# Two attentions on one core: where TensorE's waits for small transfers are placed, and the place of one PSUM bank in its ring

## The chip, the cores and the metric

The kernel runs on one core of one Trainium2 chip, in one launch. The metric is the device time of one execution in microseconds, taken as the median of several runs; lower is better. Everything is computed in float32, much of it in pairs of a high and a low part.

## The reference

Two independent attention layers over 2048 positions, with 576 channels and 32 heads of 18 channels; their outputs stand side by side in the result. A is local: each position looks at 8 keys, at distances 0, 2, ... 14. B is full.

```python
def A(x, wqkv, wo):                       # B, S, D = 1, 2048, 576;  H, Dh, W, dil = 32, 18, 8, 2
    q, k, v = split(x @ wqkv)             # each (B, H, S, Dh)
    idx = pos[:, None] - (arange(W) * dil)[None, :]
    kg, vg = k[:, :, idx], v[:, :, idx]   # (B, H, S, W, Dh), masked where idx < 0
    logits = einsum("bhsd,bhswd->bhsw", q, kg) * Dh ** -0.5
    o = einsum("bhsw,bhswd->bhsd", softmax(where(mask, logits, -1e9)), vg)
    return o.reshape(B, S, D) @ wo

def B(x, wqkv, wo):
    q, k, v = split(x @ wqkv)
    p = softmax(einsum("bhqd,bhkd->bhqk", q, k) * Dh ** -0.5)
    return einsum("bhqk,bhkd->bhqd", p, v).reshape(B, S, D) @ wo

return concatenate([A(...), B(...)], axis=-1)
```

## The kernel before

**Staging.** A first stage computes the projections of both layers (`stream`, `halves`) and leaves q, k, v in DRAM (`dqk`, `dv` for B, `da` for A). It takes the first 420 us or so (the first value product starts at 423.3). Then comes the main loop, which is 512 steps long (`ALL`) and is B's attention: 8 groups of 4 heads (`g`), in each 4 blocks of 512 queries (`b`), in each 16 tiles of 128 keys (`kt`), one step for each tile. A's local attention is done piece by piece beside the steps, and so are both output products.

**A step on TensorE.** For the four heads `h` of the group, `score` (L277) multiplies the tile's keys with the block's 512 queries into a bank of PSUM; ScalarE takes the exponential of it (L283). The scores of the step before, thus exponentiated, are then multiplied with the values by `weigh` (L748): four *value products*, one for each head, which are added up in one bank, `po`, over the 16 steps of a block.

**The maxima.** The softmax subtracts each query's maximum before the exponential. It does so inside the score itself: rows 54 and 55 of the queries' tile `qs` hold the negated maximum, in a high and a low part, and the keys have ones there. So the maxima of a block must be known before its first step, and they are computed several steps ahead (`AHEAD`) from scores of their own: 128 queries against 512 keys, which VectorE reduces. A step has room for three of these. Two are whole ones (`maximum(0)`, called A below, and `maximum(1)`, called B; matmul L157, reduction L173 or L175). The third is made of two *parts* of 256 keys each, which share a bank: D, the first part (`first_part`, L263 and L264), and E, the second. D and E lie in different halves of TensorE's rows, and before E stands a `nop` (L183) that waits for D, since both write one bank. One reduction (L190) takes both. A plain step's matmuls stand in this order: D, score 1, A, score 3, score 0, E, score 2, B, and then the four value products of the step before.

When all of a block's maxima are there, `least` takes the last reduction over them, `turn` transposes the result on VectorE one step later, `halve` splits it on GpSimd one step later into the high and low part (`mh`, `mt`), and `place` (L214 to L219) writes them, five steps later (two in the last group), into rows 54 and 55 of `qs` by eight small loads of 2 KB, first the four of `mh` (an index `j` for each), then the four of `mt`. The score that opens the block in question comes later, sometimes by a few steps and sometimes by more than a hundred.

**A beside the steps.** A's positions come in 8 tiles of 256 (`local(j)`), one every 54 steps (`GAP`) from step 10 on. GpSimd does nearly all the products, VectorE the maxima over the window (`am`, L903) and its sums. The result goes to DRAM (`dao`), and `get` (L946 to L958) loads it again, with the channels in the partitions, by six loads, as *rows* for the output product: `at0`, `at1`, `ahl`. That product, `sums_of_a`, is run 7 to 10 steps after `get`, in two halves, by `beside` (L1052), in the middle of a step's scores.

**Order.** All is issued in the order of the program (a manual schedule), so each engine runs its instructions in the order in which the Python code comes to them. `plan` and `later` put a function on the `agenda` for a step, and `due` runs it at that step's end, after the value products. A transfer is issued from SyncE's queue (`load`). Each instruction waits for what it reads and writes, and where it waits for several other queues, the additional waits stand as instructions of their own just ahead of it in its engine's queue.

**Banks.** PSUM has eight banks: `po` and seven that go round in rings (L77). In the main loop the scores use ring "scores" (banks 0 to 3), maxima and parts use ring "else" (banks 4 to 6). `bank` takes the ring's first bank and moves it to the end. So in a plain step D takes the bank that the parts had one step before, A and B theirs.

**The last group.** From step 448 on, the outputs of B's older groups are fetched back: `fetch_old` (L1015) puts eight loads of 252 KB in the queue for each of four blocks of queries, and `full` and `partial` plan the output products with them.

Of the kernel before, what the change touches and what calls it, by code (L numbers as in the profile page):

```python
# [7 lines left out]
F32 = mybir.dt.float32  # L8
# [9 lines left out]
D = 576  # L18
# [5 lines left out]
NT = S // 128  # L24
# [4 lines left out]
AB = 256  # L29
# [10 lines left out]
EARLY = 2  # L40
EARLY_PAIRS = EARLY * NB * PIECES + 2
AHEAD = 7

GAP = 54

# [14 lines left out]
def two_attentions(ctx: ExitStack, tc, xa, wa, woa, xb, wb, wob, out):  # L60
# [83 lines left out]
                for d, m in pieces or ((0, DH),) for n, i in enumerate(parts) for r in range(2)]  # L144


    def block(g, b):

        qs, ks = sets[g % 3]
        mx = maxes.tile([128, 2, 2, 4, 6], F32, name="mx", bufs=3)  # L150
        left = 2 * 8 * 6
        rest = [[(k, t, p) for k in range(NB) for t in range(4) for p in range(2)] for _ in range(2)]

        def take(ps, r, k, t, p, at, n):

            rows_ = slice(64 * r, 64 * r + 54)
            return nc.tensor.matmul(ps, qs[rows_, b, p, 128 * t : 128 * t + 128],  # L157
                                    ks[rows_, p, 512 * k + at : 512 * k + at + n], start=True, stop=True)

        def made(n):  # L160
            nonlocal left
            left -= n
            if left == 0:
                least()

        def whole(r):
            k, t, p = rest[r].pop(0)
            ps = bank()
            take(ps, r, k, t, p, 0, 512)

            def reduce():
                if k < 2:
                    nc.vector.tensor_reduce(mx[:, r, p, t, k : k + 1], ps, axis=AX.X, op=ALU.max)  # L173
                else:
                    nc.vector.tensor_reduce(mx[:, r, p, t, 2 * k - 2 : 2 * k], ps.rearrange("q (h n) -> q h n", h=2),  # L175
                                            axis=AX.X, op=ALU.max)
                made(1 + (k > 1))

            return reduce

        def part(i, k, t, p, r, ps, before=None):
            if before:
                wait = nc.tensor.nop(nofuse=True)  # L183
                tc.add_manual_dep(wait.ins, before.ins.name,
                                  mybir.DependencyInfo(mybir.DependencyClass.Sync, mybir.DependencyReason.DATA),
                                  reason="one bank")
            ins = take(ps[:, 256 * r : 256 * r + 256], r, k, t, p, 256 * i, 256)

            def reduce():
                nc.vector.tensor_reduce(mx[:, :, p, t, 2 * k - 2 + i], ps.rearrange("q (h n) -> q h n", h=2),  # L190
                                        axis=AX.X, op=ALU.max)
                made(2)

            return ins, reduce

        def least():
            m = least_rooms[n_least[0] % 2]
            n_least[0] += 1
            nc.vector.tensor_reduce(m[:, :16], mx.rearrange("q r p t k -> q (r p t) k"), axis=AX.X, op=ALU.max,
                                    negate=True)  # L200
            later(1, lambda: turn(m))

        def turn(m):

            raw = maxes.tile([128, 32], F32, name="mt", bufs=2)
            nc.vector.transpose(raw, m)
            later(1, lambda: halve(raw))

        def halve(raw):
            mh = maxes.tile([128, 32], F32R, name="mh", bufs=2)  # L210
            split_on(nc.gpsimd, mh, raw.bitcast(F32R), raw)
            later(2 if g == NG - 1 else 5, lambda: place(mh, raw))

        def place(*parts):  # L214
            placed.add((g, b))
            for k, t in enumerate(parts):
                for j in range(4):
                    load(ap(qs.bitcast(F32)[54 + k : 128 : 64, b, 0, 32 * j :], (128, 8), (1, 32)),
                         t.bitcast(F32)[32 * j : 32 * j + 16])  # L219

        return rest, whole, part

# [24 lines left out]
            n += 1  # L247

    open_parts = []

    def first_part(r):

        for i in range(2):
            given[i] += 0.5
        if open_parts:
            part, args = open_parts.pop()
        else:
            rest, _, part = blocks[find(lambda rest: rest[0] and rest[1] and rest[0][-1][0] > 1)]
            piece = rest[0].pop()
            assert rest[1].pop() == piece  # L260
            args = (0, *piece)
            open_parts.append((part, (1, *piece)))
        ps = bank()  # L263
        ins, _ = part(*args, r, ps)  # L264
        return lambda: part(*args, 1 - r, ps, ins)[1]

    e_room = None
    counted = [-1]

    def score(g, b, kt, h, also=(), kind="scores"):  # L270
# [6 lines left out]
        nc.tensor.matmul(ps, ks[at, p, 128 * kt : 128 * kt + 128], qs[at, b, p], start=True, stop=True)  # L277
# [5 lines left out]
        nc.scalar.activation(e, ps, AF.Exp, scale=SCALE)  # L283
        for reduce in reduces:
            reduce()
        return e

    vs = {}
# [98 lines left out]
    with (tc.tile_pool(name="x", bufs=1, side="right") as xp,  # L387
# [103 lines left out]
        if True:  # L491
# [231 lines left out]
            for c, b in order:  # L723
# [6 lines left out]
            turns = len(work_list) - NT + 4  # L730
            stream(work_list, lambda j: 2 * (j + 1) if j < NT - 4 else
                   few + (EARLY_PAIRS - few) * (j - NT + 5) // turns,
                   [[lambda h=h: es.append(score(0, 0, 0, h, (), "else")) for h in (r, r + 2)] for r in range(2)])
        wa_room.close()

        over, agenda = agenda, defaultdict(list)
# [1 line left out]
            plan(n - step, [(0, f) for f in fs])  # L738
        step = 0
        projecting = False  # L740


    work = ctx.enter_context(tc.tile_pool(name="work", bufs=1, reuse_waits="tile"))
    ring = "else"
    def weigh(*steps):
        for g, b, kt, es in steps:
            for i in range(4):
                nc.tensor.matmul(po[32 * i : 32 * i + 19], vs[g][:, kt, 19 * i : 19 * i + 19], es[i],  # L748
                                 start=kt == 0, stop=kt == NT - 1)
        if kt == NT - 1:  # L750
            finish(g, b)

# [109 lines left out]
    def local(j):  # L862
# [83 lines left out]
        def get(n):  # L946
            st["x"] = []
            st["n"] = n
            last = work.tile([128, 128], F32R, name="ahl", bufs=1)
            for i in range(2):  # L950
                t = work.tile([128, 4, 128], F32R, name=f"at{i}", bufs=1)
                for s in range(2):
                    load(t.bitcast(F32)[:, :, SUB * s : SUB * s + SUB],
                         dao[j, i, 2 * n + s, :512].rearrange("(c p) n -> p c n", p=128))
                load(last.bitcast(F32)[64 * i : 64 * i + 64].rearrange("p (s n) -> p s n", s=2),
                     rows(dao[j, i, 2 * n, 512], (SUB, 64), (D * SUB, 2), (1, SUB)))
# [217 lines left out]
    while step < ALL:  # L1174
        n, kt = divmod(step, NT)
        g, b = divmod(n, NB)
        many = min(4 if behind() > 0 else 3, total - int(sum(given)))
        halves_too = not inside and many in (1, 3)
        places = positions(many - halves_too)
        es = [None] * 4  # L1180
        if halves_too:
            second = first_part(0)
            order = [(1, [lambda: maximum(0)] * (many > 2)), (3, ()), (0, [second]), (2, [lambda: maximum(1)] * (many > 2))]
        else:
            order = [(h, [lambda h=h: maximum(1 - h % 2)] * (h in places)) for h in range(4)]
        for i, (h, also) in enumerate(order):

            if inside and i == (3 if 3 in places else 2):
                inside.pop(0)()
            es[h] = score(g, b, kt, h, also)  # L1190
# [43 lines left out]
```

## Time and profile before

| | |
|---|---|
| median of 3 runs | 1626.63 us (1626.19 to 1630.3) |
| the profiled execution | 1628.23 us |
| its span in the profile | 1626.5 us |
| TensorE clock granted, mean | 0.999 of full speed |
| TensorE (PE) busy | 1608.4 us, 99% of the span |
| VectorE (DVE) busy | 1396.1 us, 86% |
| ScalarE (ACT) busy | 1212.1 us, 75% |
| GpSimd (POOL) busy | 959.4 us, 59% |

The profile is of one execution; its own time stands beside its span, so that a sum made in the profile can be set against it. Matmuls and their weight loads are shown apart (PE and PEld). In lists of single instructions the first column is the start in us from the span's beginning, the second the duration; brackets at the end give the idle time of the engine ahead of the instruction, and what ended it. In the lists of waits, the row names the instruction that waited and what released it, then the idle time in us, how often, and the longest. An engine's queue (SPq, PEq) has the instructions that only issue or wait.

### The profile page before, as it was taken

Reading aid. Unit: us, or ns where it says so; the run is one execution under the profiler, and the core shown is the slowest. Engines: PE = TensorE matmul, PEld = TensorE weight load, DVE = VectorE, ACT = ScalarE, POOL = GpSimd, SP = SyncE. Lnnn points to the kernel's source line nnn. Section 1 sums busy time; section 2 is a strip of 40 time slices with the busy share of each in tenths; the row PEclk is TensorE's granted clock in tenths of the full one; section 3 lists DMA queues with packets and bytes.
Section 4 is the critical chain, followed back from the end, with each engine's and each line's share of the span. In section 5 each row is a group of like instructions: output and inputs, shape, how many; then the busy total and the mean of one; then the engine's idle time right before and its main releaser. Section 6 shows DMA issues by size and latency. Waiting matters only on the chain.

```text
span 1626.5 us, 35142 instructions
## 1 busy us (share of the span) xinstructions
PE 1608.4 (99%) x13360; PEld 944.7 (58%) x13360; DVE 1396.1 (86%) x2366; ACT 1212.1 (75%) x2419; POOL 959.4 (59%) x792
## 2 busy tenths in 40 slices
PE   9999999999999999999999999999999999999998
PEld 7999889999544444444444444444444444445676
DVE  5199999999899999999999999999999998998533
ACT  6324432121799998998998998998998997998554
POOL 2305642210265995995995995995995996930000
PEclk9999999999999999999999999999999999999999
DMA  8837954532222252254136235322532242033211
GB/s 252 235 120 197 271 166 128 134 103 78 59 56 66 72 145 61 62 127 123 40 93 142 54 93 123 93 83 73 118 98 66 52 126 61 22 116 132 94 38 59
DMA packets 186055, 172.10 MB, mean 106 GB/s; under 512 B 119152, under 2 KB 132976, under 8 KB 184160
## 3 DMA queue, kind: packets, MB, share of 16 engines
q1 hardware_dynamic: 181024, 158.31, 35.4%
q0 software_dynamic: 4032, 10.63, 3.0%
q8 instruction: 106, 1.74, 0.5%
q10 hardware_dynamic: 832, 0.92, 0.2%
q14 instruction: 61, 0.50, 0.1%
HBM read 96.94 MB, written 71.90 MB: 104 GB/s over the span
## 4 chain that ended last, share of the span: by engine, by line
PE 67%; POOL 21%; DVE 4%; DMA 4%; issue 2%; SPq 1%; ACT 1%; POOLq 0%; ACTq 0%; DVEq 0%
PE po L748 18%; PE bank L370 14%; PE bank L157 12%; PE bank L277 12%; PE bank L1052 6%; POOL pr L928 5%; PE bank L307 5%; POOL pr L885 4%; POOL pr L889 3%; POOL pr L929 3%; POOL pr L930 2%; DVE mx L173 2%; DMA dqk<-olo 1%; DVE mx L190 1%; DMA ks<-dqk 1%
## 5 line engine op out<-in xcount | busy, mean ns | idle before, releaser
L283 ACT ACTIVATE e<-bank 128x512 f32<-128x512 f32 x2048 | 1050.2, 613 | 86.3 <-PE bank L277 78.8
L157 PE MATMUL bank<-ks,qs 54*128 54x256 f32 (+1 forms) x2502 | 791.3, 382 | 9.6 <-DVE mx L190 8.1
L173 DVE TENSOR_REDUCE mx<-bank 128x1 f32<-128x512 f32 x1024 | 680.4, 684 | 88.1 <-PE bank L157 67.7
L157 PEld LDWEIGHTS bank<-ks,qs 54*128 54x128 f32 x2502 | 398.8, 184 | 442.7 <-DVE mx L190 366.2
L277 PE MATMUL bank<-qs,ks 56*128 56x512 f32 x2048 | 575.0, 426 | 0.2
L748 PE MATMUL po<-e,v 128*19 128x512 f32 x4096 | 538.3, 600 | 0.0
L175 DVE TENSOR_REDUCE mx<-bank 128x2 f32<-128x512 f32 x570 | 373.7, 685 | 34.9 <-PE bank L157 24.0
L277 PEld LDWEIGHTS bank<-qs,ks 56*128 56x128 f32 x2048 | 301.8, 185 | 49.0 <-ACT e L283 41.2
L190 DVE TENSOR_REDUCE mx<-bank 128x2 f32<-128x512 f32 x454 | 309.7, 682 | 0.0
L885 POOL TENSOR_TENSOR pr<-aq,akv 128x1024 f32<-128x1024 f32 x72 | 158.4, 2201 | 15.6 <-DMA akv<-da 13.0
L928 POOL TENSOR_TENSOR pr<-lg,akv 128x1024 f32<-128x1024 f32 x72 | 158.3, 2198 | 0.6
L889 POOL TENSOR_TENSOR pr<-pr 128x1024 f32<-128x1024 f32 x64 | 152.5, 2383 | 5.0
L748 PEld LDWEIGHTS po<-e,v 128*19 128x19 f32 x4096 | 70.6, 97 | 133.4 <-issue 124.8
L698 ACT ACTIVATE ohi<-bank 128x512 f32<-128x512 f32 (+1 forms) x56 | 30.4, 595 | 154.3 <-issue 117.1
L370 PE MATMUL bank<-xhi,ahi 64*128 64x512 f32 (+1 forms) x448 | 115.8, 390 | 0.0
L370 PE MATMUL bank<-xhi,alo 64*128 64x512 f32 (+1 forms) x448 | 110.6, 390 | 0.0
L370 PE MATMUL bank<-xlo,ahi 64*128 64x512 f32 (+1 forms) x448 | 106.8, 391 | 0.1
L929 POOL TENSOR_TENSOR pr<-pr 128x512 f32<-128x512 f32 x72 | 92.4, 1283 | 5.6
L418 POOL TENSOR_TENSOR alo<-raw,ahi 128x512 fp32r<-128x512 f32 (+1 forms) x14 | 17.6, 1258 | 122.4 <-ACT ahi L417 88.5
L510 POOL TENSOR_TENSOR olo<-olo,ohi 128x512 fp32r<-128x512 f32 x36 | 46.1, 1292 | 66.2 <-ACT ohi L509 60.6
L370 PEld LDWEIGHTS bank<-xhi,ahi 64*128 64x128 f32 (+1 forms) x448 | 63.6, 181 | 5.4
L784 POOL TENSOR_TENSOR o<-o,rec 128x512 f32<-128x512 f32 x29 | 37.3, 1287 | 49.4 <-DMA rec<-drec 26.8
(199 smaller groups left out, 1916.1 us busy)
## 6 DMA issues: line engine op xcount, KB each, us to landing
do<-n SPq DMA_DIRECT2D x28, 512.0 KB
da<-ohi SPq DMA_DIRECT2D x52, 256.0 KB
akv<-da SPq DMA_DIRECT2D x64, 175.5 KB
out<-y SPq DMA_DIRECT2D x32, 288.0 KB
qs<-dqk SPq DMA_DIRECT2D x30, 288.0 KB
ks<-dqk SPq DMA_DIRECT2D x30, 288.0 KB
at<-dao SPq DMA_DIRECT2D x64, 128.0 KB
rec<-drec SPq DMA_DIRECT2D x29, 256.0 KB
```

The costliest lines, as they stand in the source:

```text
L157: return nc.tensor.matmul(ps, qs[rows_, b, p, 128 * t : 128 * t + 128], ks[rows_, p, 512 * k + at : 512 * k + at + n], start=True, stop=True)
L173: nc.vector.tensor_reduce(mx[:, r, p, t, k : k + 1], ps, axis=AX.X, op=ALU.max)
L175: nc.vector.tensor_reduce(mx[:, r, p, t, 2 * k - 2 : 2 * k], ps.rearrange("q (h n) -> q h n", h=2), axis=AX.X, op=ALU.max)
L190: nc.vector.tensor_reduce(mx[:, :, p, t, 2 * k - 2 + i], ps.rearrange("q (h n) -> q h n", h=2), axis=AX.X, op=ALU.max)
L277: nc.tensor.matmul(ps, ks[at, p, 128 * kt : 128 * kt + 128], qs[at, b, p], start=True, stop=True)
L283: nc.scalar.activation(e, ps, AF.Exp, scale=SCALE)
L370: nc.tensor.matmul(ps, a, b, start=start, stop=stop)
L748: nc.tensor.matmul(po[32 * i : 32 * i + 19], vs[g][:, kt, 19 * i : 19 * i + 19], es[i], start=kt == 0, stop=kt == NT - 1)
L885: nc.gpsimd.tensor_mul(pr, ap(st["q"][:, 2 * c], (SUB, 2), (0, W), (1, SUB)), window(st["k"], c))
L889: nc.gpsimd.tensor_add(st["pr"], st["pr"], pr)
L928: nc.gpsimd.tensor_mul(at, ap(st["lg"], (0, 2), (SUB, W), (1, SUB)), window(st["v"], c))
L929: nc.gpsimd.tensor_add(at[:, :, :4], at[:, :, :4], at[:, :, 4:])
```

## The change

1. The waits for the loads of `place` and of `get` are put on value products. Each call appends to a queue `seen` pairs of loads with the step from which their wait may be taken: `step + SEEN`, which is 4 steps after `place`, and 5 steps after `get`. In `weigh`, the first of the four value products takes the front pair of the queue, if its step has come, and is made to wait for both loads. So each group of value products takes one pair at most, in the order in which they were asked for. The instructions that read the loaded data come after that in TensorE's queue.
2. `place` issues its eight loads as four pairs (`mh` and `mt` of one `j`, and then the next), where before it issued the four of `mh` and then the four of `mt`. `get` issues the same loads in the same order.
3. After the second part (E) is issued, the bank of the two parts is moved to the end of ring "else". In the next step D then takes the bank that A had, and A the one that the parts had; B keeps its own.
4. The order of a step is written as a string, `PLAIN` ("D1A30E2B") or one made from `positions`, instead of a list of calls that `score` runs. A reduction is now issued right behind its matmul, where before it was issued behind the exponential of the score; the matmuls stand in the order that they had.

```diff
+SEEN = 4
+PLAIN = "D1A30E2B"
...
+    seen = deque()
+    def behind_of(later, *before):
+        for b in before:
+            tc.add_manual_dep(later.ins, b.ins.name,
+                              mybir.DependencyInfo(mybir.DependencyClass.Sync, mybir.DependencyReason.DATA),
+                              reason="in order")
...
         def place(*parts):
             placed.add((g, b))
-            for k, t in enumerate(parts):
-                for j in range(4):
-                    load(ap(qs.bitcast(F32)[54 + k : 128 : 64, b, 0, 32 * j :], (128, 8), (1, 32)),
-                         t.bitcast(F32)[32 * j : 32 * j + 16])
+            for j in range(4):
+                seen.append((step + SEEN, [load(ap(qs.bitcast(F32)[54 + k : 128 : 64, b, 0, 32 * j :], (128, 8), (1, 32)),
+                                                t.bitcast(F32)[32 * j : 32 * j + 16]) for k, t in enumerate(parts)]))
...
+    parted = []
     def first_part(r):
...
         ps = bank()
+        taken = rings[ring][-1]
         ins, _ = part(*args, r, ps)
-        return lambda: part(*args, 1 - r, ps, ins)[1]
+        def second():
+            rings["else"].remove(taken)
+            rings["else"].append(taken)
+            return part(*args, 1 - r, ps, ins)[1]
+        return second
...
-    def score(g, b, kt, h, also=(), kind="scores"):
+    def score(g, b, kt, h, kind="scores"):
...
-        reduces = [beside() for beside in (also or ())]
...
-        for reduce in reduces:
-            reduce()
         return e
...
+        seen = deque((0, d) for _, d in list(seen)[4:])
...
     def weigh(*steps):
         for g, b, kt, es in steps:
             for i in range(4):
-                nc.tensor.matmul(po[32 * i : 32 * i + 19], vs[g][:, kt, 19 * i : 19 * i + 19], es[i],
-                                 start=kt == 0, stop=kt == NT - 1)
+                ins = nc.tensor.matmul(po[32 * i : 32 * i + 19], vs[g][:, kt, 19 * i : 19 * i + 19], es[i],
+                                       start=kt == 0, stop=kt == NT - 1)
+                if i == 0 and seen and seen[0][0] <= step:
+                    behind_of(ins, *seen.popleft()[1])
...
         def get(n):
...
+            moved = []
...
-                    load(t.bitcast(F32)[:, :, SUB * s : SUB * s + SUB],
+                    moved.append(load(t.bitcast(F32)[:, :, SUB * s : SUB * s + SUB],
...
             st["x"].append(last)
+            seen.extend((step + 5, moved[i : i + 2]) for i in range(0, 6, 2))
...
-        halves_too = not inside and many in (1, 3)
-        places = positions(many - halves_too)
+        if not inside and many in (1, 3):
+            order = PLAIN if many > 1 else PLAIN.replace("A", "").replace("B", "")
+        else:
+            places = positions(many)
+            order = "".join("%d%s" % (h, "BA"[h % 2] if h in places else "") for h in range(4))
...
+        for c in order:
+            if c in "0123":
+                es[int(c)] = score(g, b, kt, int(c))
+            elif c in "AB":
+                maximum("AB".index(c))()
+            elif c in "DE":
+                if parted:
+                    parted.pop()()()
+                else:
+                    parted.append(first_part("DE".index(c)))
+            else:
                 inside.pop(0)()
```

More of the change, by code (lines that the diff above doesn't have):

```diff
@@ L182, in part @@
             if before:
[L183 to L186, printed above, removed]
+                behind_of(nc.tensor.nop(nofuse=True), before)
             ins = take(ps[:, 256 * r : 256 * r + 256], r, k, t, p, 256 * i, 256)
@@ L732, in two_attentions @@
                    few + (EARLY_PAIRS - few) * (j - NT + 5) // turns,
-                   [[lambda h=h: es.append(score(0, 0, 0, h, (), "else")) for h in (r, r + 2)] for r in range(2)])
+                   [[lambda h=h: es.append(score(0, 0, 0, h, "else")) for h in (r, r + 2)] for r in range(2)])
         wa_room.close()
@@ L1177, in two_attentions @@
         many = min(4 if behind() > 0 else 3, total - int(sum(given)))
-        halves_too = not inside and many in (1, 3)
-        places = positions(many - halves_too)
-        es = [None] * 4
[L1181 to L1188, printed above, removed]
+        if not inside and many in (1, 3):
[3 more added lines that the diff above has]
+            order = "".join("%d%s" % (h, "BA"[h % 2] if h in places else "") for h in range(4))
+            if inside:
+                at = order.index("3" if 3 in places else "2")
+                order = order[:at] + "+" + order[at:]
+        es = [None] * 4
+        for c in order:
[9 more added lines that the diff above has]
+            else:
                 inside.pop(0)()
-            es[h] = score(g, b, kt, h, also)
         for fs in (behind_scores, outside):
```

6 lines of the change are left out of this document (3 added, 3 removed).

## The prediction, made before the changed kernel was run

> **What bounds the kernel now.** I read the page first, then the waits, then the timeline of single steps, and last the transfer queue beside the steps in which the change puts its waits.
>
> ```profile
> span 1626.5 us, 35142 instructions
> PE 1608.4 (99%) x13360; PEld 944.7 (58%) x13360; DVE 1396.1 (86%) x2366; ACT 1212.1 (75%) x2419; POOL 959.4 (59%) x792
> ...
> PEclk9999999999999999999999999999999999999999
> ...
> PEld bank L157 <- DVE mx L190: 366.2, 420, 3.3
> ...
> DVE am L903 <- POOL lg L892: 5.9, 5, 1.9
> ...
> PE bank L157 <- DVE mx L190: 8.1, 7, 2.4
> ```
>
> TensorE (PE, with its weight loads PEld) is busy 99% at full clock, so what delays it delays the end. The 366.2 us look like a prize: 420 times the weight load that opens a step (the first of the two parts, piece D) ends its idle time on VectorE's reduction of the parts. The timeline says how much of that is real.
>
> ```profile
> 1441.28 0.18 PEld L157 LDWEIGHTS bank<-ks,qs 54*128 54x128 f32 x1 [0.85 <-DVE mx L190]
> ...
> 1441.39 0.19 PEld L157 LDWEIGHTS bank<-ks,qs 54*128 54x128 f32 x1
> ...
> 1442.34 0.14 PEld L748 LDWEIGHTS po<-e,v 128*19 128x19 f32 x8 [0.25 <-issue]
> 1442.34 1.05 PE L748 MATMUL po<-e,v 128*19 128x512 f32 x8
> 1442.54 0.68 DVE L190 TENSOR_REDUCE mx<-bank 128x2 f32<-128x512 f32 x1
> 1443.14 0.68 DVE L173 TENSOR_REDUCE mx<-bank 128x1 f32<-128x512 f32 x1
> 1443.32 0.18 PEld L157 LDWEIGHTS bank<-ks,qs 54*128 54x128 f32 x1 [0.85 <-DVE mx L190]
> ...
> 1443.94 0.18 PEld L157 LDWEIGHTS bank<-ks,qs 54*128 54x128 f32 x1
> ...
> 1444.37 0.14 PEld L748 LDWEIGHTS po<-e,v 128*19 128x19 f32 x8 [0.25 <-issue]
> 726.88 0.18 PEld L277 LDWEIGHTS bank<-qs,ks 56*128 56x128 f32 x1 [0.85 <-ACT e L283]
> ```
>
> A plain step lasts 2.03 us (1442.34 to 1444.37): 0.98 of value products, then 1.05 of scores and maxima. The reduction that D waits for ended at 1443.22, 0.10 before D's load. And in the last row a step opens with a score, which waits for no reduction: the same 0.85. So these 0.85 are the array finishing its value products; the reduction is merely the latest event inside them. Where it really is late, the matmul idles too: 8.1 us, 7 times, in the fence above.
>
> **The bank at the end of its ring.** In the built order of both kernels the matmuls stand alike. Only the banks change: D now needs the bank that A filled one step before (reduced first), A needs that of the parts (reduced second), B its own as ever. In a plain step this saves nothing, by the 0.85. Where a reduction is late, look at the worst kind:
>
> ```profile
> 867.86 0.14 PEld L748 LDWEIGHTS po<-e,v 128*19 128x19 f32 x8 [0.24 <-issue]
> 870.42 0.18 PEld L157 LDWEIGHTS bank<-ks,qs 54*128 54x128 f32 x1 [2.43 <-DVE mx L190]
> 868.74 0.42 DVE L903 TENSOR_TENSOR am<-lg 128x256 f32<-128x256 f32 x1 [1.43 <-POOL lg L892]
> 869.68 0.68 DVE L190 TENSOR_REDUCE mx<-bank 128x2 f32<-128x512 f32 x1
> 870.28 0.68 DVE L175 TENSOR_REDUCE mx<-bank 128x2 f32<-128x512 f32 x1
> ```
>
> VectorE stood 1.43 us for GpSimd and all three reductions came late. D could start 0.6 earlier, but A would then wait to 870.42, and B, last before the value products, needs the third reduction: not before 870.96, as now. The price is between 0 and the 8.1 us of the waits; I take 0.3 gained, because B's wait is next late.
>
> **Waits taken off the readers.** In the built order the waits that stand as instructions of their own fall from 59 to 10 ahead of scores (L277), from 36 to 3 inside A's output sums (L1052), and rise from 2 to 157 ahead of value products (L748). What one costs:
>
> ```profile
> 451.81 0.14 PEld L748 LDWEIGHTS po<-e,v 128*19 128x19 f32 x8 [0.25 <-issue]
> 452.80 0.18 PEld L157 LDWEIGHTS bank<-ks,qs 54*128 54x128 f32 x1 [0.85 <-DVE mx L190]
> 453.15 0.18 PEld L277 LDWEIGHTS bank<-qs,ks 56*128 56x128 f32 x1 [0.16 <-issue]
> 454.15 0.14 PEld L748 LDWEIGHTS po<-e,v 128*19 128x19 f32 x8 [0.24 <-issue]
> L277 PEldq EVENT_SEMAPHORE  x59: 51/51/51, 415.1 to 1552.4; - x59
> L748 PEldq EVENT_SEMAPHORE  x2: 51/51/51, 556.4 to 840.3; - x2
> 556.86 0.14 PEld L748 LDWEIGHTS po<-e,v 128*19 128x19 f32 x8 [0.24 <-ACT o L757]
> ```
>
> Four of them between D's load (452.80) and the score's (453.15) make this step 2.34 instead of 2.03: 0.30 us. Thirteen blocks start so; eleven lose all four and one two of them: 11.5 x 0.30 = 3.5 us at most. But GpSimd makes VectorE late five times (the "am" row); a gain in the stretch of GpSimd work before such a place is only waited for there. By the times of the thirteen starts four lie in such stretches and two just ahead of the transfers below, which hang on GpSimd too. I count 5.5 of them: 1.7 us. A's sums gain at most 33 x 0.051 = 1.7, half of it hidden likewise, and take over the rows that land late: 0.5.
>
> **Waits put on value products.** The extra 155 cost 155 x 0.051 = 7.9 us if nothing hides them, and nothing if the 0.25 of idle time before each group of products does. The nearest row is the one at 556.86: such a wait stood before it, and its idle time is 0.24, as without. I take 0. Behind a wait that is not yet satisfied, though, stands all of TensorE: scores, maxima, and so ScalarE and VectorE. A pair of transfers must now have landed 4 steps (rows: 5) after it was asked for, although the score that reads it may be 100 steps off. I followed the order of the waits to their value products and looked when their transfers can be there.
>
> ```profile
> 1430.19 7.47 SPq L1015 DMA_DIRECT2D qs<-do  x8
> 1437.79 0.38 SPq L943 DMA_DIRECT2D dao<-ao  x1
> 1438.28 4.36 SPq L218 DMA_DIRECT2D qs<-mh  x4
> SPq L218 <- DMA qs<-do: 4.8, 6, 0.9
> GB/s 0 304 424 396 88 143 168 127 147 127 119 127 127 172 131 143 172 346 407 428 212 168 160 184 176 180 176 172 184 180 194 196 184 97 34 4 0 0 20 2
> 1165.82 2.45 SPq L218 DMA_DIRECT2D qs<-mh  x4
> GB/s 117 59 181 345 316 152 98 115 148 147 164 116 55 123 204 172 147 94 123 164 242 254 254 147 98 180 197 107 82 98 82 102 102 94 51 11 3 0 4 5
> 1173.00 0.14 PEld L748 LDWEIGHTS po<-e,v 128*19 128x19 f32 x8 [0.25 <-issue]
> 719.81 1.05 PE L748 MATMUL po<-e,v 128*19 128x512 f32 x8
> 713.93 1.03 SPq L953 DMA_DIRECT2D at<-dao  x2
> 736.00 1.62 SPq L953 DMA_DIRECT2D at<-dao  x2
> 746.78 1.05 PE L748 MATMUL po<-e,v 128*19 128x512 f32 x8
> ```
>
> The two GB/s rows are the transfer view of 1430 to 1450 and of 1157 to 1177, 0.5 us a slice. In the first, eight loads of 252 KB (qs<-do) and a store of 576 KB are issued from 1430.19, the maxima of a late block from 1438.28; the queue runs until slice 33 to 35, 1446.5 to 1447.5, and the maxima's own issues wait six times for qs<-do. The product that now waits for the first pair stood at 1442.34: 4.2 to 5.2 us late. I take 5.1, the queue's last bytes. In the second the queue runs dry between 1174.0 and 1175.5; the product at 1173.00 waits 1.0 to 2.5, and I take 2.3. Twice it is A's rows: issued at 713.93 and 736.00, waited for at 719.81 and 746.78. If they take the 9 us of the maxima (1438.28 to 1447.5), they land 3 late and 2 early; I take 1.2 and 0.7, between nothing and these. The stall at 1173.00 gives something back: GpSimd, which does not wait for TensorE there, makes VectorE late 60 us on, and that lateness, about 0.9, is gone (bounds 0 and 1.9, the longest of the "am" row).
>
> By the Trainium skill, "DMA: Bandwidth & Descriptors", section "Anatomy of one DMA — SWDGE (gpsimd) path", a DMA takes a fixed 2.0 us or so and its bytes over 436 GB/s. These 2 KB would then be there at 1440.5, the stall would be nil and the sum -2.5 us. The rows here speak against it: the queue still moves 160 to 200 GB/s at 1446. The same page, section "Queues, rings and completion order", has each engine take its descriptors in ring order, which fits.
>
> **The sum.** -0.3 (bank), -1.7 and -0.5 (readers), 0 (satisfied waits), +5.1 +2.3 +1.2 +0.7 (transfers), -0.9 (given back): +5.9 us. The profiled execution took 1628.23 us (span 1626.5), so it would take 1634.1; the median of the runs, 1626.63, lies 1.6 lower, so I forecast 1632.5.
>
> **Rivals.**
> (1) The transfers are there in time: another order of the rings' work lands the small ones early. Then only gains stay, -2.5 us: 1624.1; with no gain lost to GpSimd -5.5: 1621.1, faster than before. For it: most maxima are read long after they land. Against: the two GB/s rows. It decides from the point where the maxima issued at 1438.28 land by 1442.3.
> (2) The reduction is what holds the step. If D's load, free of it, came up to 0.06 us sooner in 420 steps, that is 25 us: 1601. The row at 726.88 speaks against it.
> (3) The new waits do not hide: 155 x 0.051 = 7.9 on top of +5.9, 1640.4. Against it stands the row at 556.86, one case only.
>
> **Chances.** Forecast 0.67, (1) 0.18, (2) 0.05, (3) 0.10. About 0.3% (4.9 us) is what a measurement of this kernel can tell from no change. The forecast's own bounds run from about +1 (4.2 + 1.0 + 0 for the transfers, gains in full: 0.3 + 3.5 + 0.5) to +10 (5.2 + 2.5 + 3.0, nothing given back, 0.7 of gains); I put 0.12 of its 0.67 inside 0.3%. So slower 0.55 + 0.10 = 0.65; within 0.25, with 0.13 of (1); faster 0.05 + 0.05 = 0.10. The range 1626.5 to 1637.0 holds the forecast's bounds and leaves out (2), (3) and most of (1).
>
> **What would show it.** Right: the value products near 1442 and 1173 show idle times of some 5 and 2 us ended by the maxima's DMA, those near 720 and 747 about 1 by A's rows; the row "PEld bank L157 <- DVE mx L190" shrinks while plain steps stay at 2.03; block starts lose their 2.34. Wrong: plain steps below 2.0 (rival 2), idle time before value products of 0.30 where a wait stands (rival 3), or no idle time over 1 us before any value product (rival 1).

## The result and the profile after

| | before | after |
|---|---|---|
| median | 1627.89 us (4 runs, 1626.19 to 1630.3) | 1638.05 us (4 runs, 1636.2 to 1639.09) |
| the profiled execution | 1628.23 us | 1637.17 us |
| its span | 1626.5 us | 1635.4 us |
| TensorE clock granted, mean | 0.999 | 0.996 |

The ratio of after to before is 1.0055, with a 95% interval of 1.0042 to 1.0068: 9 us slower. Between the two profiled executions lie 8.9 us.

The page of the kernel after, its first lines:

```profile
span 1635.4 us, 35211 instructions
...
PE 1610.9 (99%) x13360; PEld 949.9 (58%) x13360; DVE 1395.6 (85%) x2366; ACT 1212.3 (74%) x2419; POOL 959.3 (59%) x792
```

The engines are as busy as before; the span is longer. Rows of its waits (idle time in us, how often, the longest):

```profile
PEld bank L170 <- DVE mx L200: 341.2, 406, 0.8
PEld po L762 <- issue: 121.0, 482, 0.4
...
PEld bank L170 <- DVE mx L186: 28.4, 32, 3.2
...
PEld po L762 <- DMA qs<-mh: 8.9, 3, 6.1
...
PE po L762 <- DMA qs<-mt: 8.0, 3, 5.8
```

The value products (now L762) wait for the maxima three times, once for 6.1 us; no such row was there before. Most of the value products still open with 0.25 us of idle time (121.0 over 482, before 124.8 over 495), although 157 waits of their own now stand ahead of them. The row of D (now L170) still names the parts' reduction (now L200) 406 times, although D no longer needs it: in a plain step it is only the latest event. Where VectorE is late, D now waits for A's reduction (L186), for up to 3.2 us, where it was 3.3 for the parts'.

This is the long wait, in the timeline of the kernel after: the queue of transfers, the value products, D's load.

```profile
1432.29 6.45 SPq L1033 DMA_DIRECT2D qs<-do  x8
...
1439.72 0.64 SPq L227 DMA_DIRECT2D qs<-mh  x1
1440.57 0.57 SPq L227 DMA_DIRECT2D qs<-mt  x1
...
1441.70 0.14 PEld L762 LDWEIGHTS po<-e,v 128*19 128x19 f32 x8 [0.25 <-issue]
1442.69 0.18 PEld L170 LDWEIGHTS bank<-ks,qs 54*128 54x128 f32 x1 [0.85 <-DVE mx L200]
1449.61 0.19 PEld L762 LDWEIGHTS po<-e,v 128*19 128x19 f32 x8 [6.12 <-DMA qs<-mh]
1449.64 1.92 PE L762 MATMUL po<-e,v 128*19 128x512 f32 x8 [5.83 <-DMA qs<-mt]
1451.49 0.28 PEld L170 LDWEIGHTS bank<-ks,qs 54*128 54x128 f32 x1 [1.69 <-issue]
...
1453.28 1.84 PE L762 MATMUL po<-e,v 128*19 128x512 f32 x8
1455.05 0.18 PEld L170 LDWEIGHTS bank<-ks,qs 54*128 54x128 f32 x1 [1.61 <-DVE mx L186]
...
1456.10 1.05 PE L762 MATMUL po<-e,v 128*19 128x512 f32 x8
```

The first pair of maxima was asked for behind eight loads of 252 KB and a store, and let the products go at 1449.61. The step from 1441.70 to 1449.61 took 7.91 us, 5.87 more than in the profile of before. Then comes what the prediction did not have: the products now take 1.92 us and 1.84 instead of 1.05, and D's weight load 0.28 instead of 0.18, until 1455. The windows of the kernel after show why. Behind the length stand the busy times of PE, PEld, DVE, ACT and POOL, then the granted clock, the share of the DMA engines and GB/s.

```profile
1445.00:1447.00 2.00, 0.00 (x0) 0.00 (x0) 0.23 (x1) 0.29 (x1) 0.00 (x0) 1.00 0.46 170
1447.00:1449.00 2.00, 0.00 (x0) 0.00 (x0) 0.00 (x0) 0.00 (x0) 0.00 (x0) 0.77 0.34 130
1449.00:1451.00 2.00, 1.36 (x8) 0.19 (x8) 0.00 (x0) 0.00 (x0) 0.00 (x0) 0.50 0.03 4
1451.00:1453.00 2.00, 2.00 (x12) 1.35 (x8) 0.47 (x1) 0.68 (x2) 0.00 (x0) 0.50 0.61 133
1453.00:1455.00 2.00, 2.00 (x10) 0.16 (x8) 1.42 (x3) 1.39 (x3) 0.00 (x0) 0.52 0.69 152
1455.00:1457.00 2.00, 2.00 (x20) 0.84 (x16) 1.30 (x3) 1.40 (x3) 0.00 (x0) 1.00 0.62 216
...
624.00:626.00 2.00, 1.60 (x14) 0.43 (x11) 0.27 (x1) 2.00 (x6) 1.62 (x2) 1.00 0.23 80
626.00:628.00 2.00, 1.09 (x7) 0.67 (x7) 2.00 (x5) 1.21 (x4) 0.00 (x0) 1.00 0.38 123
628.00:629.00 1.00, 1.00 (x12) 0.32 (x9) 1.00 (x3) 1.00 (x3) 0.00 (x0) 0.95 0.41 126
629.00:630.00 1.00, 1.00 (x10) 0.12 (x2) 1.00 (x3) 0.55 (x2) 0.00 (x0) 0.50 0.91 207
...
632.00:633.00 1.00, 1.00 (x16) 1.00 (x14) 0.27 (x2) 0.00 (x0) 0.94 (x2) 0.84 0.03 4
```

While TensorE stood, its granted clock fell to 0.50, and it stayed there: by the rows for 0.92 + 4 + 1.92 = 6.8 us. The two steps behind the stall lost 1.63 and 0.79 us, 2.4 together. A second stretch of half clock lies at 629, for 0.10 + 3 + 0.32 = 3.4 us, behind a place where VectorE came late for GpSimd; it cost 1.5. The Trainium skill, "TensorE: Matmul & The Clock Gate", Part 1, section "What's actually happening", says that the clock is halved after an idle window and comes back after a busy one, and that the windows are 3.413 us long and run freely. The lengths agree (one and two windows). The traces also show what share of a window matters. In every kept profile the changes of the clock lie whole multiples of 3.413 us apart; the two stretches here start 819.2 us apart, which is 240 windows. These are three windows of this grid in the kernel after, the first of them just ahead of the stretch at 629:

```profile
625.48:628.90 3.42, 2.11 (x19) 0.99 (x16) 3.17 (x7) 2.63 (x6) 0.22 (x1) 1.00 0.43 146
1171.62:1175.03 3.41, 3.09 (x23) 1.28 (x20) 2.70 (x6) 3.37 (x8) 3.25 (x4) 1.00 0.32 100
1175.03:1178.44 3.41, 1.94 (x16) 0.87 (x16) 1.41 (x3) 1.58 (x4) 3.17 (x4) 1.00 0.07 13
```

And these are two of the kernel with the large loads asked for later (below), around its wait near 1173:

```profile
1171.34:1174.75 3.41, 1.34 (x14) 0.63 (x14) 1.89 (x3) 2.31 (x5) 3.33 (x3) 1.00 0.13 44
1174.75:1178.16 3.41, 3.41 (x20) 1.51 (x16) 1.37 (x3) 1.59 (x4) 3.25 (x5) 0.50 0.03 3
```

In the kernel after, the wait of 2.1 us that ended at 1176.46 fell into two windows, which stayed busy for 3.09 and 1.94 us, and full clock went on. In the other kernel a wait of 2.4 us at the same place fell into one, 1.34 us busy, and half clock followed. Over the thirteen kept profiles (past their first 20 us), all 19 windows at full clock with TensorE busy for less than 47% were followed by half clock, 4 of the 32 windows with 47 to 68% were, and none with more. So a stop need not be full, and a short one can be enough; what decides between 47 and 68% stays open.

The other places where value products wait, by the timeline of the kernel after:

```profile
713.30 0.17 PEld L762 LDWEIGHTS po<-e,v 128*19 128x19 f32 x8 [0.67 <-DMA qs<-mh]
...
722.23 0.16 PEld L762 LDWEIGHTS po<-e,v 128*19 128x19 f32 x8 [1.01 <-DMA at<-dao]
...
749.91 0.14 PEld L762 LDWEIGHTS po<-e,v 128*19 128x19 f32 x8 [0.92 <-DMA at<-dao]
...
1176.46 0.16 PEld L762 LDWEIGHTS po<-e,v 128*19 128x19 f32 x8 [2.08 <-DMA qs<-mh]
```

With the value products of the two profiles side by side, step by step, the steps before these four lost 0.42, 0.74, 0.67 and 1.83 us, and the reader behind the third gained 0.69. Twelve block starts gained 3.8 in sum. The account of the 8.9 us: 5.87 for the stall at 1442, 2.42 and 1.50 for half clock, 1.83 for the stall at 1173, 1.14 for the three smaller ones less their reader, less 3.77 at block starts and 0.95 given back at 1236. That is 8.0; some 0.9 remains for VectorE's other late places and for differences that were there before the main loop.

### The profile page after: what moved, and what is told of

Same layout as the page of the kernel before. It is cut to its first block, busy times and chain, and to the rows that moved or that the text cites. A ratio compares the mean times of both kernels' runs of the same rounds, so it can differ in the third digit from the quotient of the medians.

```text
span 1635.4 us, 35211 instructions
## 1 busy us (share of the span) xinstructions
PE 1610.9 (99%) x13360; PEld 949.9 (58%) x13360; DVE 1395.6 (85%) x2366; ACT 1212.3 (74%) x2419; POOL 959.3 (59%) x792
## 4 chain that ended last, share of the span: by engine, by line
PE 61%; POOL 27%; DMA 5%; DVE 3%; issue 2%; SPq 1%; ACT 1%; POOLq 0%; ACTq 0%; DVEq 0%
PE po L762 15%; PE bank L383 14%; PE bank L170 10%; PE bank L294 9%; POOL pr L944 7%; PE bank L1070 6%; PE bank L320 5%; POOL pr L945 4%; POOL pr L901 4%; POOL pr L905 3%; POOL pr L946 2%; POOL ao L947 1%; DMA out<-y 1%; DMA qs<-mt 1%; DMA at<-dao 1%
## 5 line engine op out<-in xcount | busy, mean ns | idle before, releaser
L170 PE MATMUL bank<-ks,qs 54*128 54x256 f32 (+1 forms) x2502 | 792.5, 383 | 6.9 <-DVE mx L186 5.3
L186 DVE TENSOR_REDUCE mx<-bank 128x1 f32<-128x512 f32 x1024 | 680.4, 684 | 97.2 <-PE bank L170 78.1
L170 PEld LDWEIGHTS bank<-ks,qs 54*128 54x128 f32 x2502 | 399.0, 184 | 442.3 <-DVE mx L200 341.2
L762 PE MATMUL po<-e,v 128*19 128x512 f32 x4096 | 539.5, 601 | 9.3 <-DMA qs<-mt 8.0
L200 DVE TENSOR_REDUCE mx<-bank 128x2 f32<-128x512 f32 x454 | 309.5, 682 | 0.0
L762 PEld LDWEIGHTS po<-e,v 128*19 128x19 f32 x4096 | 70.7, 97 | 142.6 <-issue 121.0
L105 POOL CAST mh<-mt 128x32 fp32r<-128x32 f32 x32 | 6.7, 210 | 105.7 <-DVE mt L216 105.7
```

The costliest lines, as they stand in the source:

```text
L762: ins = nc.tensor.matmul(po[32 * i : 32 * i + 19], vs[g][:, kt, 19 * i : 19 * i + 19], es[i], start=kt == 0, stop=kt == NT - 1)
```

## The experiments

Theory 1: the loss is made of transfers that land late at a value product, and of the half clock behind the stall. Theory 2: it is the bank's move, since D and A now need other reductions. All times are medians, and each ratio is to the kernel before.

**The two parts apart.** First the bank's move alone, with the waits at their readers:

```diff
-            for j in range(4):
-                seen.append((step + SEEN, [load(... mh, mt of j ...)]))
+            for k, t in enumerate(parts):
+                for j in range(4):
+                    load(...)
...
-            seen.extend((step + 5, moved[i : i + 2]) for i in range(0, 6, 2))
```

> The bank's move alone: the waits for the maxima and the rows sit on their readers again, and the loads are issued in their old order. Theory 1 (the loss is made of transfers that land late at a value product, and of the half clock that a long stall brings): within 1.5 us of before, and no value product waits over 0.5 us for a transfer; the step at 1442 keeps 2.03 us. Theory 2 (the loss comes from the bank's move, because D now needs the reduction of A, and A that of the parts): 5 us or more slower than before, spread over the steps in which VectorE is late and those with A's sums.

Measured: 1626.15 us, ratio 0.9989 (0.9980 to 0.9998). Then the waits alone:

```diff
         def second():
-            rings["else"].remove(taken)
-            rings["else"].append(taken)
             return part(*args, 1 - r, ps, ins)[1]
```

> The waits alone: the pairs of transfers are waited for at value products as in the change, but the bank stays where it was in its ring. Theory 1: 7 to 10 us slower than before, with a stall of 5 to 6 us near 1442 and weight loads of 0.28 instead of 0.18 us behind it. Theory 2: less than 4 us slower.

Measured: 1639.06 us, ratio 1.0065 (1.0053 to 1.0078). Theory 2 is out: the bank's move by itself makes the kernel a little faster, and the waits bring the whole loss. In the timeline of the kernel with the waits alone stand the stall and the first step at half clock behind it (3.66 us instead of 2.03); at 1173 that kernel lost another 3.4 us to a stall:

```profile
1451.75 0.19 PEld L760 LDWEIGHTS po<-e,v 128*19 128x19 f32 x8 [6.19 <-DMA qs<-mh]
1455.41 0.16 PEld L760 LDWEIGHTS po<-e,v 128*19 128x19 f32 x8 [0.44 <-issue]
```

**One wait out of 157.** The bank's move, and of all waits on value products only that for the first pair of maxima of the late block:

```diff
+                if j == 0 and not projecting and step == STEPS * (NG - 1) + 6:
                     seen.append((step + SEEN, pair))
```

> The bank's move, and one single wait on a value product: the first pair of maxima of the late block, at the place where the changed kernel stalls near 1442. Theory 1 (this one transfer, and the half clock behind its stall, make most of the loss): the stall of 5 to 6 us and two to four steps at half clock are there, 8 us more than the bank's move alone, so 4 to 7.5 us slower than before. Its rival (the loss is spread over the 157 waits): within 2 us of the bank's move alone, so no slower than before.

Measured: 1631.6 us, ratio 1.0029 (1.0019 to 1.0039). Its waits have one row of the kind,

```profile
PEld po L764 <- DMA qs<-mh: 6.4, 1, 6.4
```

and its timeline shows the place, with a step of 3.46 us behind the stall:

```profile
1443.91 0.19 PEld L764 LDWEIGHTS po<-e,v 128*19 128x19 f32 x8 [6.44 <-DMA qs<-mh]
1447.37 0.14 PEld L764 LDWEIGHTS po<-e,v 128*19 128x19 f32 x8 [0.25 <-issue]
```

Against the bank's move alone this one wait costs 1.0029 - 0.9989 = 0.40%, 6.5 us, where 8 were expected (7.6 us by the steps of its profile: 6.2 for the stall and 1.4 for half clock). The whole of the waits cost 1.0055 - 0.9989 = 0.66%, 10.7 us. So one wait makes some 60% of it; each ratio is uncertain by about 0.1%, so the share is rough.

**The transfers ahead of it.** The whole change, with the eight large loads asked for 8 steps later:

```diff
-            plan(STEPS * g, [(4, lambda: fetch_old(0)), (24, lambda: fetch_old(1)), ...
+            plan(STEPS * g, [(12, lambda: fetch_old(0)), (24, lambda: fetch_old(1)), ...
```

> The whole change, but the first eight loads of 252 KB of the last group are asked for 8 steps later, so the maxima of the late block are issued ahead of them. Theory 1: the stall near 1442 is gone with its half clock, 7 to 9 us less than the changed kernel, so 0 to 2.5 us slower than before. Theory 2: the maxima's place in the queue doesn't matter, within 2 us of the changed kernel. A third possibility is that the eight loads now delay the rows of A's last tile, which are asked for two steps ahead of them; then half of the gain or more is lost again in a wait for at<-dao.

Measured: 1629.14 us, ratio 1.0015 (1.0003 to 1.0027), 0.40% under the changed kernel. The timeline:

```profile
1438.52 0.57 SPq L227 DMA_DIRECT2D qs<-mh  x1
1439.17 0.55 SPq L227 DMA_DIRECT2D qs<-mt  x1
...
1444.14 0.14 PEld L762 LDWEIGHTS po<-e,v 128*19 128x19 f32 x8 [0.25 <-issue]
...
1448.98 6.66 SPq L1033 DMA_DIRECT2D qs<-do  x8
```

The product that stalled (at 1444.14 here) does not wait any more. The same loads of 2 KB, asked for ahead of the large ones, are there in time; the place in the queue made them late. The rest of its loss sits at 1173 (2.1 us, and 1.5 for a stretch of half clock), at the rows near 717 (1.1), and at 1356 to 1368 (1.4), where half clock lasted two windows. A third possibility, that the large loads would now delay the rows of A's last tile, did not come: no step behind 1440 lost over 0.1 us.

**Half clock or late data.** The changed kernel, with 24 matmuls ahead of the stalling product whose result nobody reads:

```diff
         for g, b, kt, es in steps:
+            if step == STEPS * (NG - 1) + 10:
+                ps = bank()
+                rings["else"].insert(0, rings["else"].pop())
+                for _ in range(24):
+                    nc.tensor.matmul(ps, sets[g % 3][0][:54, b, 0, :128], sets[g % 3][1][:54, 0, :512], start=True, stop=True)
```

> The changed kernel with 24 matmuls more, whose result nobody reads, just ahead of the value product that stalls near 1442: TensorE works while the transfers land. Theory 1 with the clock (the array's idle time itself brings the half clock): the stall is filled by some 5 to 6 us of matmuls, the granted clock stays at 1.00, the value products behind it take 1.05 us again, and the time is 1.5 to 3 us under the changed kernel, though it does more work. Its rival (what is slow behind the stall is the landing transfers or late exponentials): the products behind it take 1.9 us again, and the time is that of the changed kernel or above it.

Measured: 1634.85 us, ratio 1.0053 (1.0039 to 1.0066). By the ratio it can't be told from the changed kernel, where 1.5 to 3 us less were expected; this profile has half clock at another place, behind a longer stall at 1173. At the place in question its timeline and its windows are plain:

```profile
1442.63 5.73 PE L765 MATMUL bank<-ks,qs 54*128 54x512 f32 x24 [0.28 <-DVE mx L186]
...
1448.29 1.05 PE L768 MATMUL po<-e,v 128*19 128x512 f32 x8
```

```profile
1447.00:1449.00 2.00, 2.00 (x15) 0.90 (x13) 0.00 (x0) 0.00 (x0) 0.00 (x0) 1.00 0.07 18
1449.00:1451.00 2.00, 2.00 (x20) 0.84 (x16) 1.07 (x2) 1.19 (x3) 0.00 (x0) 1.00 0.46 99
```

With TensorE kept busy the clock stays at 1.00, and the products behind take 1.05 again. The place cost 6.0 us in this profile, the stall alone, against 8.3 in the changed kernel. So it is TensorE's idle time, and not the landing data, that slows what follows.

**More time for the transfers.** The change with SEEN = 8 in place of 4, once with A's rows at their readers (the second line of the diff) and once with the rows at value products:

```diff
-SEEN = 4
+SEEN = 8
...
-            seen.extend((step + 5, moved[i : i + 2]) for i in range(0, 6, 2))
```

> The change with SEEN = 8 instead of 4, so that a pair of maxima must have landed 8 steps after it was asked for, and with A's rows waited for by their readers as before. Theory 1: no value product waits over 0.5 us for a transfer, the block starts keep what they gained, so 1 to 4 us faster than before. Theory 2: 2 us or more slower than before, since the bank is still moved.

Measured: 1625.65 us, ratio 0.9985 (0.9976 to 0.9993).

> The change with SEEN = 8 and A's rows still waited for at value products. Theory 1: the stalls near 1442 and 1173 are gone, those of the rows near 710, 718 and 747 remain with 1.1 to 1.5 us in sum, so 0.5 to 2 us slower than the same kernel with the rows at their readers, and within 2 us of before. Its rival (the rows' waits are hidden, since their readers would have waited anyway): the same time as with the rows at their readers, and no idle time over 0.5 us before a value product.

Measured: 1626.06 us, ratio 0.9990 (0.9980 to 0.9999). The first has no wait of a value product for a transfer left; the second still has this row:

```profile
PEld po L762 <- DMA at<-dao: 3.1, 4, 1.5
```

Theory 1 holds: four steps more, and the loss becomes a small gain, no more than the bank's move alone brought (0.9989). What the rows cost lies inside the intervals (0.4 us between the medians); the stalls are there, but the step at 625, which lost 0.8 us with the rows at their readers, gained 0.2 with them at value products, behind a stall of 0.9 at 595.

**What a block's start costs.** The bank's move alone had one surprise. Its scores still have all 59 waits of their own (the row of the line's instructions), and yet the block starts lost their 0.3 us (the timeline):

```profile
L295 PEldq EVENT_SEMAPHORE  x59: 51/51/51, 414.1 to 1548.5; - x59
```

```profile
450.69 0.14 PEld L763 LDWEIGHTS po<-e,v 128*19 128x19 f32 x8 [0.24 <-issue]
...
452.72 0.13 PEld L763 LDWEIGHTS po<-e,v 128*19 128x19 f32 x8 [0.24 <-issue]
```

2.03 us, where the same step took 2.34 before. Theory 3: the waits themselves are short, but they stand behind D in the queue, and D's own wait ended late. With the bank moved, D waits for an older reduction, and the queue works the four waits off while the array still finishes the value products. A test with the old bank and no wait on a value product, where the waits for the block's maxima, the eight loads of `place`, stand on D:

```diff
         ins, _ = part(*args, r, ps)
+        if not projecting and step % NT == 0:
+            for x in loads[divmod(step // NT, NB)]:
+                tc.add_manual_dep(ins.ins, x.ins.name, ...)
```

> Before, with the bank where it was and no wait on a value product; only the waits for a block's maxima are put on D, the matmul that opens the block's first step, instead of on the score behind it. Theory 3 (what costs 0.3 us at a block's start is that the waits stand behind D, whose own wait for the parts' reduction ends late, so that they are worked off one after another once D is let go): the block starts take 2.03 to 2.10 instead of 2.34 us and the time is 1 to 3.5 us under before, as with the bank's move alone. Its rival (such waits cost their 0.05 us each wherever they stand inside a step): the block starts keep 2.3 us or take more, and the time is that of before or above it.

Measured: 1626.78 us, ratio 0.9995 (0.9986 to 1.0003). In its timeline:

```profile
450.76 0.14 PEld L755 LDWEIGHTS po<-e,v 128*19 128x19 f32 x8 [0.25 <-issue]
...
452.80 0.14 PEld L755 LDWEIGHTS po<-e,v 128*19 128x19 f32 x8 [0.25 <-issue]
```

The waits are the same four instructions as before, each for two transfers; only their place is another (the score's line has 9 such instructions instead of 59, D's 73 instead of 23). The block starts take 2.04, so theory 3 is right on its mechanism. The traces agree for this block: before, the parts' reduction ends at 452.70 and the four waits begin at 452.75, beside D's load; with the bank moved, A's reduction ends at 450.98 and they begin at 451.03, 0.6 us ahead of D's load. The time did not follow as expected: steps at 625, 990, 1112 and 1233 waited 2.4 us longer for VectorE, and this profile has three stretches of half clock, where that of before has one.

**Where the gains go.** Theory 4: what is gained is waited for where VectorE is late for GpSimd (`am`), so plan A's tails later. Three kernels: before with everything from `am` on 2 steps later, the bank's move alone with the same, and the bank's move with 1 step. The diff shows the first line of it; all later pieces of the tail are moved alike.

```diff
-        pieces = [(33, lower), (35, exponents), (39, share), (60, upper), ...
+        pieces = [(35, lower), (37, exponents), (41, share), (62, upper), ...
```

> Before, without any part of the change; of A's tiles, everything from the maximum over the window (am) on is planned 2 steps later, so that GpSimd's logits are there when VectorE comes to them. Theory 4 (VectorE's waits for GpSimd at am, and the half clock that follows some of them, cost time at five places, by the profile of before 1.1, 1.6, 1.5, 1.0 and 2.9 us beside one stretch of half clock with 1.5 us): these waits are gone, no half clock before the end, 5 to 9 us faster than before. Its rival (GpSimd is as late at whatever comes next): within 2 us of before.

> The bank's move alone, with the same 2 steps as the kernel sent with it. Theory 4: nothing is waited away any more ahead of the am places, so the bank's move now brings its 13 x 0.31 = 4.0 us in full: 3 to 4.5 us faster than the same shift without the bank's move. Its rival (the bank's move costs something of its own where VectorE is late or in the steps with A's sums): 2.5 us or less.

> The bank's move alone, with A's tails planned 1 step later instead of 2. Theory 4: one step is 2.03 us and covers four of the five places, so within 2 us of the kernel with 2 steps. Its rival (two steps push GpSimd into the next tile): faster than with 2 steps by over 2 us.

Measured: 1634.16 us, ratio 1.0041 (1.0029 to 1.0054); 1634.05 us, 1.0042 (1.0030 to 1.0055); 1625.1 us, 0.9989 (0.9980 to 0.9998). Theory 4's remedy fails. For the first kernel neither the theory (5 to 9 us faster) nor its rival (within 2 us) said so much loss; for the other two the rivals were right. With 2 steps the five late places became clean, and GpSimd was late again at three of the new ones. Here is the worst, first in the timeline of the kernel before, then in that with 2 steps:

```profile
1356.27 0.85 DVE L903 TENSOR_TENSOR am<-lg 128x256 f32<-128x256 f32 x1 [1.93 <-POOL lg L892]
```

```profile
1361.99 0.85 DVE L903 TENSOR_TENSOR am<-lg 128x256 f32<-128x256 f32 x1 [2.29 <-POOL lg L892]
```

So planning A's tails later does not by itself take the lateness away. Beside that, with 2 steps and the old bank, one step with A's sums near 730 took 3.9 us longer: it waited 2.0 us for A's rows and then ran at half clock. One near 1495 took 8.8 us, since its maxima landed late: A's rows, and eight large loads behind them, had moved (these from 1472.99 to 1479.09), and the maxima behind those were asked for at 1489.26 instead of 1482.95. The bank's gain, expected to be 3 us or more here, did not show in the times (0.9989 with one step is what it was with none), although the block starts of the profiles show it 0.3 us at a time. With no shift, the profile of the bank's move alone shows where a part of it goes: the steps at 625, 1112, 1233 and 1355 lost 0.84, 0.27, 0.51 and 0.32 us. What became of the rest stays open.

## Why the prediction was right, and where it was wrong

The forecast was 5.9 us slower, 1632.5; measured is 0.55% slower. On the median of the three runs that the prediction had, the ratio gives 1635.6, inside its range; the median of the four runs after, 1638.05, lies 1 us above the range's upper end.

- **The late transfers**: right in mechanism, places and size. +9.3 was forecast for four places; measured are 5.9 + 1.8 + 1.8 = 9.5 for the stalls themselves, at five. The place at 1442 was 0.8 more than its 5.1: the large loads were asked for 2.1 us later (1432.29 against 1430.19), and the product would without the wait have come only 1.4 us later (1441.70 + 2.03 = 1443.73 against 1442.34). That at 1173 was 0.5 less. Near 710 it was a pair of maxima that came late, where I had expected only A's rows, from 720 on.
- **Half clock**: the term that the sum lacked, and the reason why 5.9 became 8.9. It measured 2.4 us behind the stall at 1442 and 1.5 at 629. The prediction quoted the row of the granted clock, all nines, and read from it that the clock is not in play; but a slice there is 41 us long, and a stretch of 3.4 us hides in it. The profile of before has one such stretch itself, at 1359. That 8.9 still lies near 5.9 is in part luck: against these 3.9 us stand 2.1 more from block starts than the sum counted.
- **Satisfied waits at nothing**: right. 157 of them left the idle time ahead of value products at 0.25, and rival (3) falls.
- **The bank at -0.3, the readers at -1.7**: wrong in who earns it. Either part by itself takes the 0.3 us off a block's start, and both together no more than one. The step that failed is "the reduction is merely the latest event inside them": that holds for D's matmul, but the queue behind D stands until the reduction ends, and what else is in the queue then comes too late. Gross, the block starts gave 3.8, near the prediction's 3.5 at most, where its sum counted 1.7; and gains ahead of late GpSimd were waited for, as at 625, where the step took 3.89 instead of 3.13.
- **Given back**: right. The step at 1233 went from 2.99 to 2.04, 0.95 against 0.9. In the four kernels with the bank moved and no stall at 1173 (bank alone, one wait, and the two with SEEN = 8) the same step lost 0.5 to 0.7 instead.
- **Rivals**: (1) fails at the point that it named: the first pair landed at 1449.6 and not by 1442.3. The fixed 2 us of the Trainium skill, "DMA: Bandwidth & Descriptors", section "Anatomy of one DMA — SWDGE (gpsimd) path", which the prediction weighed there, are given for DMAs issued from GpSimd. These loads are issued from SyncE, and behind the large loads the pair took 8.5 us from the end of its issue (1440.57 + 0.57) to the product; asked for ahead of them it was there within 4.4 (1439.72 to 1444.14). (2) fails: plain steps stayed at 2.03 to 2.04.

## What to carry to other kernels

A wait that was met cost nothing here, where its engine stood anyway; one that was not met held up every engine behind it, for 5.87 us at the worst. So put waits early only for transfers whose worst case has been looked up, and look it up by what stands ahead of them in their queue, not by their bytes: a margin of 8 steps instead of 4, with the rows left at their readers, turned a loss of 0.55% into a gain of 0.15%. When a stall of TensorE is priced, add the half clock behind it: in this kernel 1.4 to 2.8 us for a stall of 6, and nothing or 1.5 us for one of 2, as it fell into two windows of the clock or into one.

A wait that "costs nothing" because its instruction could not start earlier can still hold up the queue behind it. Look at what stands next in the queue before you call it free.

## What the runs showed that I had not expected

- The granted clock goes to 0.50 for one or more stretches of 3.4 us, in every profile of this kernel but one, and at changing places: at 1359 before; at 629 and 1448 after; at three places in the kernel with the waits on D and at none before the end with SEEN = 8 and the rows at value products. The stretch at the very end, which every profile has, is left out of this. A stretch cost 0.8 to 1.5 us where the same steps could be set beside full clock. At 1359 it cost nothing that can be seen: VectorE was busy all through it, and the step took 5.29 us with it (before) and 5.70 without (after). The kernel before ran between 1625.2 and 1632.4 us over all experiments, and this may be a part of that spread; it wasn't shown.
- It needs no full stop: TensorE was busy for 2.11 of the 3.42 us ahead of the stretch at 629, while a stop of 2.1 us at 1176 in the same profile, which two windows shared, brought none.
- Waits that stand as instructions of their own take 51 ns each, but only the place of the queue decides whether that is seen: four of them cost 0.31 us behind a late D, and the same four ahead of it nothing.
